# Attention score products on 64 rows each, with q stored without zero padding

## The chip, the cores and the metric

The kernel runs on one core of a Trainium2 chip. The metric is device time in microseconds, from the first to the last instruction of one execution. The kernel before was run three times; the median is 1041.5 us. TensorE is called PE in the rows, its weight loads PEld, VectorE DVE, ScalarE ACT, GpSimd POOL, and the engine that issues the transfers SP.

## The reference, cut to what matters

Two batches with eight heads of 576 tokens and 64 dimensions go through two attentions that are added: one over tokens averaged in fours (144 of them), one local, in which a token sees those less than four positions away. Two layers of expert products follow.

```python
q_d = q.reshape(B, H, Sd, factor, D).mean(axis=3)      # k_d, v_d in the same way
out_d = sm_attn(q_d, k_d, v_d)                         # softmax(scale * q k^T) v
out_up = np.repeat(out_d, factor, axis=2)
mask = np.abs(pos[:, None] - pos[None, :]) < factor
scores = np.where(mask, scale * np.matmul(q, k.transpose(0, 1, 3, 2)), -1000000000.0)
...
x = attn_out.transpose(0, 2, 1, 3).reshape(B * S, H * D)
x = _moe_ref(x=x, **moe_kwargs)                        # silu(x @ w_gate) * (x @ w_val) @ w_out
return _moe2_ref(x=x, **moe2_kwargs)                   # eight experts, routed by a balanced softmax
```

## The kernel before, in words

**The attention** (L362 to L517) works on eight pairs of heads. A pair fills the 128 partitions: the even head has partitions 0 to 63 of q and k (transposed, 576 columns), the odd head 64 to 127. `load_pair` (L309) loads k into one of three buffers and q into one of three fixed tiles `qz`. Such a tile has room for two copies of the 576 columns: copy 0 holds the even head and zeros in partitions 64 to 127, copy 1 the odd head and zeros in partitions 0 to 63. The zeros are written once, by six memsets on GpSimd (L111, L112); each load writes the two other quarters with a transfer of its own (L313, L314).

`pooled` (L369) scales k on ScalarE (L373) and sums k and q over groups of four tokens on VectorE (L374, L381); since q's tile holds two copies, its sum reads 1152 columns.

`scores(h)` (L392) takes two PSUM banks for a head. A product with an identity first writes the mask into each bank (L397, L402). Five window products of 128 by 128 are added to it (L400, L404), with q as the stationary operand: all 128 partitions of copy j, so the other head's half of k meets zeros. Two products of 72 rows with the pooled k follow (L406). All these products but the mask are fp32. Then VectorE takes the extreme of each row (L409 to L411), ScalarE the exponential with its sum (L415 to L421), VectorE the reciprocals (L423, L424), and GpSimd scales the rows (L426, L428). `turn(h)` (L431) transposes the result on TensorE (L437 to L441) and ScalarE copies it out (L443 to L445). `combine(pr)` (L448) multiplies with the values of both heads (L457, L465), adds the upsampled part (L468, L474) and splits the sum into two 16-bit parts (helper L165 to L170). Scores, transposes and combine share six PSUM banks, two for each of them at a time.

**The order.** The generator in L481 to L517 writes it down: scores of the first four heads; then for each head its transposes, the scores of the head four further on, and behind each odd head the combine. The loads of the pair three further on come behind the odd head's scores (L489, L490). From this order and the dependencies a scheduler makes each engine's list at build time by modelled durations, so an engine may take a later instruction first; on the chip each engine follows its list. Transfers are all issued by SP, in one list. Those of gate weights and of pooled values are tied behind the last load of q (`gate(loaded[-1])`, L215, L321).

**Around it** the first layer's weights arrive as 64-bit floats, whose words VectorE and ScalarE turn into fp32 (L189) and then into two 16-bit parts. `conv_gv`, `prep_gv` and three early steps of gate/value products (`gv_step`) are put between the heads (L673 to L682); the rest of that layer follows, and then the eight experts. All products of those layers are issued in L177.

Of the kernel before, what the change touches and what calls it, by code (L numbers as in the profile page):

```python
# [7 lines left out]
F32 = mybir.dt.float32  # L8
# [4 lines left out]
ALU = mybir.AluOpType  # L13
AX = mybir.AxisListType
# [3 lines left out]
B, H, S, D = 2, 8, 576, 64  # L18
FAC, SD = 4, 144
# [3 lines left out]
P = 128  # L23
NPAIR = 4
HS = SD // 2
# [3 lines left out]
WSTART = (0, 120, 240, 360, 448)  # L29
WCUT = (0, 124, 244, 364, 484, 576)  # L30
NW = 5
# [6 lines left out]
DW = 2 * SD  # L38
# [12 lines left out]
NQ = 3  # L51
V4B = 4
NSHORT = NPAIR
QDV = (0, 1, 2, 3, 4, 5, 6, 7)
# [4 lines left out]
def tile_kernel(ctx, tc, qT, kT, vw, vd4, wgv, wo, wg2, w1, w2, out):  # L59
    nc = tc.nc  # L60
    V, A, G, T = nc.vector, nc.scalar, nc.gpsimd, nc.tensor
# [7 lines left out]
    ap = ctxA.enter_context(tc.tile_pool(name="ap", bufs=2, side="right"))  # L69
# [28 lines left out]
    identb = ap.tile([P, P], BF16, tag="identb", bufs=1, name="identb")  # L98
    V.tensor_scalar(identb, dist, 0.0, None, op0=ALU.is_equal)
    maskb = ap.tile([P, 4, P], BF16, tag="maskb", bufs=1, name="maskb")  # L100
# [1 line left out]
                    op0=ALU.is_ge, op1=ALU.mult)  # L102
    ident = cp.tile([P, P], F32, name="ident")
    built.append(V.tensor_scalar(ident, dist, 0.0, None, op0=ALU.is_equal))
    qz = [ap.tile([P, 2, S], F32, tag=f"qz{i}", bufs=1, name=f"qz{i}") for i in range(NQ)]
    vz = [ap.tile([P, NW, 2, P], F32, tag=f"vz{i}", bufs=1, name=f"vz{i}") for i in range(2)]
    vdz = [ap.tile([HS, 2, 2, P], F32, tag=f"vdz{i}", bufs=1, name=f"vdz{i}") for i in range(2)]
    stm = [ap.tile([P, 8], F32, tag=f"stm{i}", bufs=1, name=f"stm{i}") for i in range(2)]
    sts = [ap.tile([P, 8, 2], F32, tag=f"sts{i}", bufs=1, name=f"sts{i}") for i in range(2)]
    for i in range(NQ):  # L110
        G.memset(qz[i][64:, 0], 0.0)  # L111
        G.memset(qz[i][:64, 1], 0.0)  # L112
    for i in range(2):
        V.memset(stm[i], 0.0)
        V.memset(sts[i][:, :, 0], 1.0)
# [190 lines left out]
    ld = {}  # L306
    loaded = []

    def load_pair(pr):  # L309
        k = ap.tile([P, S], F32, tag="k", bufs=NQ, name=f"k{pr}")  # L310
        nc.sync.dma_start(k, kT[pr])
        q = qz[pr % NQ]
        nc.sync.dma_start(q[:64, 0], qT[pr, :64])  # L313
        loaded.append(nc.sync.dma_start(q[64:, 1], qT[pr, 64:]))  # L314
        ld[pr] = k

    v4s = {}
# [44 lines left out]
    def attention():  # L362

        def bank(nm):
            return [psa.tile([P, 512], F32, tag="att", bufs=6, name=f"{nm}_{i}") for i in range(2)]

        qd, kd, exs, ats = {}, {}, {}, {}

        def pooled(pr):  # L369
            q, k = qz[pr % NQ], ld[pr]  # L370
            qd[pr] = ap.tile([P, 2, SD], F32, tag="qd", name=f"qd{pr}")
            kd[pr] = ap.tile([P, SD], F32, tag="kd", name=f"kd{pr}")
            A.activation(k, k, AF.Copy, scale=-0.125)  # L373
            V.tensor_reduce(kd[pr], k.rearrange("p (s a) -> p s a", a=FAC), axis=AX.X, op=ALU.add)  # L374
            A.activation(kd[pr], kd[pr], AF.Copy, scale=1.0 / (FAC * FAC))
            if pr not in QDV:
                t = ap.tile([P, 2, 2 * SD], F32, tag="qt", bufs=1, name=f"qt{pr}")
                G.tensor_tensor(t, q[:, :, 0::2], q[:, :, 1::2], op=ALU.add)
                G.tensor_tensor(qd[pr], t[:, :, 0::2], t[:, :, 1::2], op=ALU.add)
            else:  # L380
                V.tensor_reduce(qd[pr], q.rearrange("p j (s a) -> p j s a", a=FAC), axis=AX.X, op=ALU.add)  # L381

        def pooled_v(pr):
            v4, vd = v4s[pr], vdz[pr % 2]
# [3 lines left out]
            for j in range(2):  # L388
                h = slice(64 * j, 64 * j + 64)
                G.tensor_tensor(vd[:, :, j, h], vt[:, 0, :, h], vt[:, 1, :, h], op=ALU.add)  # L390

        def scores(h):  # L392
            pr, j = h // 2, h % 2
            q, k = qz[pr % NQ], ld[pr]
            nm = f"{h}"
            ps = bank(f"s{nm}")
            T.matmul(ps[0], lhsT=identb, rhs=maskb.rearrange("p u w -> p (u w)"), start=True, stop=False)  # L397
            for w in range(NW - 1):
                ws = slice(WSTART[w], WSTART[w] + P)
                T.matmul(ps[0][:, w * P:(w + 1) * P], lhsT=q[:, j, ws], rhs=k[:, ws],  # L400
                         start=False, stop=w == NW - 2)
            T.matmul(ps[1][:, DW:DW + P], lhsT=identb, rhs=maskb[:, 0], start=True, stop=False)  # L402
            ws = slice(WSTART[4], WSTART[4] + P)
            T.matmul(ps[1][:, DW:DW + P], lhsT=q[:, j, ws], rhs=k[:, ws], start=False, stop=True)  # L404
            for t in range(2):
                T.matmul(ps[1][:HS, t * SD:(t + 1) * SD], lhsT=qd[pr][:, j, t * HS:(t + 1) * HS],  # L406
                         rhs=kd[pr], start=True, stop=True)
            mx, sm = stm[h % 2], sts[h % 2]
            V.tensor_reduce(mx[:, :4], ps[0].rearrange("p (u w) -> p u w", u=4), axis=AX.X, op=ALU.min)  # L409
            V.tensor_reduce(mx[:, 4:5], ps[1][:, DW:DW + P], axis=AX.X, op=ALU.min)  # L410
            V.tensor_reduce(mx[:HS, 5:7], ps[1][:HS, :DW].rearrange("p (u w) -> p u w", u=2),  # L411
                            axis=AX.X, op=ALU.min)
            ex = ap.tile([P, NW * P + DW], F32, tag="ex", bufs=6, name=f"ex{nm}")
            for w in range(4):
                A.activation(ex[:, w * P:(w + 1) * P], ps[0][:, w * P:(w + 1) * P], AF.Exp, scale=-1.0,  # L415
                             bias=mx[:, w:w + 1], accum_out=sm[:, w, 0:1])
            A.activation(ex[:, DO - P:DO], ps[1][:, DW:DW + P], AF.Exp, scale=-1.0,
                         bias=mx[:, 4:5], accum_out=sm[:, 4, 0:1])
            for t in range(2):
                A.activation(ex[:HS, DO + t * SD:DO + (t + 1) * SD], ps[1][:HS, t * SD:(t + 1) * SD], AF.Exp,  # L420
                             scale=-1.0, bias=mx[:HS, 5 + t:6 + t], accum_out=sm[:HS, 5 + t, 0:1])  # L421
            rs = ap.tile([P, 8], F32, tag="rs", name=f"rs{nm}")
            V.tensor_reduce(rs, sm, axis=AX.X, op=ALU.add)  # L423
            V.reciprocal(rs, rs)  # L424
            x = ex[:, :DO].rearrange("p (w k) -> p w k", w=NW)
            G.tensor_tensor(x, x, rs[:, :NW, None].to_broadcast([P, NW, P]), op=ALU.mult)  # L426
            x = ex[:HS, DO:].rearrange("p (t k) -> p t k", t=2)
            G.tensor_tensor(x, x, rs[:HS, 5:7, None].to_broadcast([HS, 2, SD]), op=ALU.mult)  # L428
            exs[h] = ex
# [53 lines left out]
        def start(h):  # L483
            if h < NH:
                if h % 2 == 0:
                    with tc.issue_after(built[0].ins), tc.issue_after(built[1].ins):
                        pooled(h // 2)
                scores(h)
                if h % 2 and h // 2 + NQ < NPAIR * B:  # L489
                    load_pair(h // 2 + NQ)  # L490
# [8 lines left out]
        for h in range(NH):  # L499
# [4 lines left out]
            if h % 2:  # L504
                pr = h // 2
# [157 lines left out]


    load_pair(0)
    load_pair(1)
    load_pair(2)
    load_v(0)
# [4 lines left out]
    for n, _ in enumerate(attention()):  # L673
        pr, r = divmod(n - AHEAD - 5, 6)
        if n == AHEAD:
            conv_gv(0)
        if r == 0 and pr >= 0:
            if pr in EARLY:
                gv_step(0, EARLY.index(pr), True)
            if pr % 2:  # L680
                prep_gv(pr // 2, x1_done[pr])
                conv_gv(pr // 2 + 1, x1_done[pr])  # L682
# [179 lines left out]
```

## Time and profile before

| | us |
|---|---|
| median of 3 runs | 1041.5 |
| lowest and highest | 1039.41 and 1043.37 |
| span of the profiled execution | 1041.1 |
| PE busy in it | 1013.4 |
| DVE busy in it | 756.6 |
| ACT busy in it | 457.7 |
| POOL busy in it | 81.3 |

The profiled execution's own time is the span, from its first to its last instruction. A busy time is the union of an engine's instructions. Matmuls overlap, so that distances between their starts say more of PE's pace than their durations. In the rows, L400 is line 400 of the kernel before, `s<-k,qz` an instruction that writes tile s and reads k and qz, `x8` a count; `<-` behind an idle time names what ended it.

### The profile page before, as it was taken

What the parts mean: (1) busy time and instruction counts of PE and PEld (TensorE: products, weight loads), DVE (VectorE), ACT (ScalarE), POOL (GpSimd) and SP (SyncE); (2) the same over time, 40 slices, a digit from 0 to 9 for tenths busy, and PEclk for the clock granted to TensorE, in tenths of its full rate; (3) what the DMA queues carried; (4) which work ended last, traced back from release to release, by engine and by line L of the source; (5) the groups of instructions that cost most, each with busy time, mean ns of one, the idle gap of its engine ahead of it and who ended that gap; (6) DMA issues with size and microseconds to landing.
All of it is one profiled execution on the core that took longest, in us unless ns stands there. A gap on an engine that the chain in (4) does not pass through costs nothing.

```text
span 1041.1 us, 16454 instructions
## 1 busy us (share of the span) xinstructions
PE 1013.4 (97%) x6540; PEld 651.0 (63%) x6541; DVE 756.6 (73%) x1555; ACT 457.7 (44%) x957; POOL 81.3 (8%) x117
## 2 busy tenths in 40 slices
PE   5989899999999999999999999999999999999998
PEld 4978465666577756566655755656565575665644
DVE  6787888965683999797679749749866973974721
ACT  6797576656351746235135215413522631441300
POOL 5664000000000200000000000000000000000000
PEclk8999899999999999999999999999999999999999
DMA  9542242330020022013012110201201211020011
GB/s 213 156 145 68 81 163 92 151 122 1 1 81 2 1 82 95 28 41 122 1 41 82 41 41 16 107 1 41 96 27 41 81 42 41 1 82 1 1 41 51
DMA packets 22459, 65.54 MB, mean 63 GB/s; under 512 B 12080, under 2 KB 12336, under 8 KB 15984
## 3 DMA queue, kind: packets, MB, share of 16 engines
q1 hardware_dynamic: 22384, 64.51, 18.1%
q8 instruction: 51, 0.84, 0.3%
q14 instruction: 24, 0.20, 0.1%
HBM read 62.14 MB, written 2.36 MB: 62 GB/s over the span
## 4 chain that ended last, share of the span: by engine, by line
PE 85%; DVE 7%; DMA 3%; ACT 3%; issue 1%; SPq 0%; ACTq 0%; DVEq 0%
PE y L177 36%; PE p L177 30%; PE gv L177 10%; PE wo L177 4%; DMA rawg<-in_wgv 2%; PE s L400 1%; PE o L465 1%; DMA k<-in_kT 1%; DVE w L170 1%; DMA rawo<-in_wo 1%; PE lgps L593 1%; DVE cvg L204 0%; DVE mxw L146 0%; PE o L457 0%; PE t L437 0%
## 5 line engine op out<-in xcount | busy, mean ns | idle before, releaser
L177 PE MATMUL y<-w,hhl 128*128 128x512 f16 (+1 forms) x1752 | 396.2, 376 | 0.0
L177 PE MATMUL p<-bop,w 128*128 128x320 f16 (+1 forms) x2688 | 354.4, 286 | 0.8 <-DVE u L734 0.7
L177 PEld LDWEIGHTS <-w 128*128 128x128 f16 x2688 | 263.0, 98 | 90.6 <-issue 1.3
L177 PEld LDWEIGHTS <-hhl 128*128 128x128 f16 x1752 | 171.5, 98 | 178.1
L762 ACT ACTIVATE hhl<-h 128x640 f16<-128x640 f32 (+1 forms) x128 | 83.3, 676 | 159.9 <-DVE h L734 159.8
L177 PE MATMUL gv<-xhl,gv 128*128 128x320 f16 (+1 forms) x864 | 144.3, 329 | 2.9 <-ACT gv L169 2.3
L169 ACT ACTIVATE w<-r,s_w 128x256 f16<-128x256 f32 (+1 forms) x96 | 71.2, 783 | 118.0 <-PE y L177 86.3
L177 PEld LDWEIGHTS <-gv 128*128 128x128 f16 x864 | 84.9, 99 | 58.8 <-issue 3.5
L793 DVE SCALAR_TENSOR_TENSOR acc<-y,pe,acc 128x512 f32<-128x512 f32 (+1 forms) x64 | 47.3, 739 | 101.3 <-PE y L177 100.5
L763 DVE SCALAR_TENSOR_TENSOR hhl<-h,hhl 128x640 f16<-128x640 f32 (+1 forms) x128 | 94.4, 752 | 15.3 <-ACT hhl L762 14.0
L734 DVE SCALAR_TENSOR_TENSOR h<-p,u 128x256 f32<-128x256 f32 (+1 forms) x192 | 84.9, 452 | 19.8 <-PE p L177 14.1
L170 DVE SCALAR_TENSOR_TENSOR w<-r,s_w,w 128x256 f16<-128x256 f32 (+1 forms) x96 | 78.0, 831 | 16.8 <-ACT w L169 16.7
L177 PE MATMUL wo<-ahl,wo 128*128 128x320 f16 (+1 forms) x432 | 73.9, 333 | 0.0
L169 ACT ACTIVATE w<-cmb,s_w 128x512 f16<-128x512 f32 x64 | 43.0, 710 | 42.1 <-DVE cmb L274 40.0
L177 PEld LDWEIGHTS <-wo 128*128 128x128 f16 x432 | 43.3, 101 | 28.2
L734 DVE SCALAR_TENSOR_TENSOR u<-p,u 128x320 f32<-128x320 f32 (+1 forms) x128 | 57.2, 447 | 4.1 <-PE p L177 3.2
L156 POOL PARTITION_ALL_REDUCE g_w<-gm_w x16 | 6.3, 392 | 592.7 <-DVE gm_w L152 586.8
L751 ACT ACTIVATE s<-p 128x256 f32<-128x256 f32 (+1 forms) x64 | 25.4, 397 | 56.9 <-PE p L177 56.9
L146 DVE TENSOR_REDUCE mxw<-r 128x1 f32<-128x1024 f32 x32 | 37.4, 1213 | 12.8 <-DMA r<-in_w 12.8
L170 DVE SCALAR_TENSOR_TENSOR w<-cmb,s_w,w 128x512 f16<-128x512 f32 x64 | 45.9, 739 | 0.1
L294 ACT ACTIVATE j<-r 128x1024 f16<-128x1024 f32 x32 | 33.4, 1045 | 24.5 <-DMA r<-in_w 24.5
L170 DVE SCALAR_TENSOR_TENSOR ahl<-act,sc,ahl 128x512 f16<-128x512 f32 (+1 forms) x24 | 19.6, 818 | 17.6 <-ACT ahl L169 17.6
(203 smaller groups left out, 937.9 us busy)
## 6 DMA issues: line engine op xcount, KB each, us to landing
r<-in_w SPq DMA_DIRECT2D x32, 1024.0 KB, 4.8
rawg<-in_wgv SPq DMA_DIRECT2D x12, 1024.0 KB, 4.8
rawo<-in_wo SPq DMA_DIRECT2D x6, 1024.0 KB, 6.3
vz<-in_vw SPq DMA_DIRECT2D x16, 160.0 KB, 3.2
k<-in_kT SPq DMA_DIRECT2D x8, 288.0 KB, 4.3
qz<-in_qT SPq DMA_DIRECT2D x16, 144.0 KB, 5.2
v<-in_vd SPq DMA_DIRECT2D x8, 288.0 KB
out<-acc SPq DMA_DIRECT2D x8, 256.0 KB, 2.0
```

The costliest lines, as they stand in the source:

```text
L146: V.tensor_reduce(o, i, axis=axis, op=ALU.max, apply_absolute_value=True)
L169: return (A.activation(hi, src, AF.Copy, scale=s), V.scalar_tensor_tensor(lo, src, s, hi, op0=ALU.mult, op1=ALU.subtract))
L170: V.scalar_tensor_tensor(lo, src, s, hi, op0=ALU.mult, op1=ALU.subtract))
L177: T.matmul(ps, lhsT=wf(i, k), rhs=xf(j, k), start=n == 0, stop=n == 3 * nk - 1)
L294: A.activation(junk, t[:, 2 * j:2 * j + 2].rearrange("p a n -> p (a n)"), AF.Abs, accum_out=mx[:, 2 * i + j:2 * i + j + 1])
L400: T.matmul(ps[0][:, w * P:(w + 1) * P], lhsT=q[:, j, ws], rhs=k[:, ws], start=False, stop=w == NW - 2)
L465: T.matmul(dst, lhsT=v[:, w, j], rhs=ats[2 * pr + j][:, off:off + hi - lo], start=j == 0, stop=j == 1)
L734: V.scalar_tensor_tensor(o, ps, HSC, u, op0=ALU.mult, op1=ALU.add)
L751: A.activation(s1, p1, AF.Copy, scale=HSC)
L762: ra = A.activation(t[:, 0], h, AF.Relu)
L763: rv = V.scalar_tensor_tensor(t[:, 1], h, 0.0, t[:, 0], op0=ALU.max, op1=ALU.subtract)
L793: V.scalar_tensor_tensor(acc[t][:, ds], ps, p[:, t:t + 1], acc[t][:, ds], op0=ALU.mult, op1=ALU.add)
```

## The change

A q tile loses its second copy and its zeros, and one transfer loads both heads. The sum over four tokens reads 576 columns. The products of a pair's two heads are issued together, ahead of the even head's softmax: the masks of both heads, then window by window the even head's product on partitions 0 to 63 and the odd head's on 64 to 127, each into its own head's bank, then the pooled products in the same way. The pair takes four banks at once. The softmax of each head stays where it was.

```diff
-    qz = [ap.tile([P, 2, S], F32, tag=f"qz{i}", bufs=1, name=f"qz{i}") for i in range(NQ)]
+    qz = [ap.tile([P, S], F32, tag=f"qz{i}", bufs=1, name=f"qz{i}") for i in range(NQ)]
...
-    for i in range(NQ):
-        G.memset(qz[i][64:, 0], 0.0)
-        G.memset(qz[i][:64, 1], 0.0)
...
-        nc.sync.dma_start(q[:64, 0], qT[pr, :64])
-        loaded.append(nc.sync.dma_start(q[64:, 1], qT[pr, 64:]))
+        loaded.append(nc.sync.dma_start(q, qT[pr]))
...
-            qd[pr] = ap.tile([P, 2, SD], F32, tag="qd", name=f"qd{pr}")
+            qd[pr] = ap.tile([P, SD], F32, tag="qd", name=f"qd{pr}")
...
+            V.tensor_reduce(qd[pr], q.rearrange("p (s a) -> p s a", a=FAC), axis=AX.X, op=ALU.add)
...
+        def products(pr):
+            q, k = qz[pr % NQ], ld[pr]
+            pss = [bank(f"s{2 * pr + j}") for j in range(2)]
+            hd = [slice(64 * j, 64 * j + 64) for j in range(2)]
+            for ps in pss:
+                T.matmul(ps[0], lhsT=identb, rhs=maskb.rearrange("p u w -> p (u w)"), start=True, stop=False)
+            for ps in pss:
+                T.matmul(ps[1][:, DW:DW + P], lhsT=identb, rhs=maskb[:, 0], start=True, stop=False)
+            for w in range(NW):
+                ws = slice(WSTART[w], WSTART[w] + P)
+                for ps, h in zip(pss, hd):
+                    o = ps[0][:, w * P:(w + 1) * P] if w < 4 else ps[1][:, DW:DW + P]
+                    T.matmul(o, lhsT=q[h, ws], rhs=k[h, ws], start=False, stop=w > 2)
+            for t in range(2):
+                for ps, h in zip(pss, hd):
+                    T.matmul(ps[1][:HS, t * SD:(t + 1) * SD], lhsT=qd[pr][h, t * HS:(t + 1) * HS],
+                             rhs=kd[pr][h], start=True, stop=True)
+            return pss
+
         def scores(h):
-            pr, j = h // 2, h % 2
...
+            pr = h // 2
+            if h % 2 == 0:
+                pss[pr] = products(pr)
+            nm, ps = f"{h}", pss[pr][h % 2]
```

## Rows read from the trace of the kernel before

**Rows 1.** the profile's page, part 1: busy us, share of the span, instructions

```profile
PE 1013.4 (97%) x6540; PEld 651.0 (63%) x6541; DVE 756.6 (73%) x1555; ACT 457.7 (44%) x957; POOL 81.3 (8%) x117
```

**Rows 2.** by stretch: busy us of PE, PEld, DVE, ACT, POOL; granted clock; DMA share; GB/s

```profile
0.00:28.00 28.00, 15.92 (x89) 12.93 (x90) 17.23 (x45) 17.94 (x76) 17.15 (x35) 0.88 0.92 210
28.00:66.00 38.00, 33.77 (x324) 31.67 (x324) 29.77 (x71) 32.10 (x132) 22.03 (x26) 1.00 0.57 160
66.00:108.40 42.40, 42.40 (x332) 35.68 (x331) 33.89 (x85) 34.15 (x125) 22.80 (x25) 1.00 0.24 74
108.40:142.00 33.60, 28.39 (x168) 16.93 (x167) 28.94 (x54) 21.12 (x32) 1.97 (x3) 0.90 0.33 125
...
331.00:1041.00 710.00, 705.93 (x4470) 437.15 (x4468) 514.81 (x1064) 252.34 (x424) 12.19 (x21) 1.00 0.12 46
```

**Rows 3.** chain of waits, 0 to 28 us: start, us, what

```profile
11.51 7.18 DMA k<-in_kT
19.22 9.03 DMA rawg<-in_wgv
```

**Rows 4.** chain of waits, 66 to 108.4 us, its shares by line

```profile
by line: PE gv L177 24.5%; PE o L465 21.8%; PE s L400 11.0%; PE o L457 10.6%; PE t L437 8.9%; PE s L406 6.1%; PE t L441 4.8%; PE s L404 3.3%; PE s L397 2.9%; PE t L438 2.1%; DVE act L554 1.8%; PE sm_gv L162 1.5%; PE sm_gv L160 1.2%; PE sm_v
```

**Rows 5.** PE's groups by line, 28 to 108.4 us; last row 66 to 108.4

```profile
L400 PE MATMUL s<-k,qz 128*128 128x128 f32 x88 | 11.8, 275 | 0.1
...
L400 PE MATMUL s<-k,qz 128*128 128x128 f32 x40 | 5.5, 276 | 0.0
```

**Rows 6.** PE in order of time, 66 to 76 us: start, us, instructions merged

```profile
65.88 1.05 PE L400 MATMUL s<-k,qz 128*128 128x128 f32 x8
66.77 0.22 PE L402 MATMUL s<-maskb,identb 128*128 128x128 bf16 x1
66.82 0.44 PE L404 MATMUL s<-k,qz 128*128 128x128 f32 x2
67.10 0.65 PE L406 MATMUL s<-kd,qd 128*72 128x144 f32 x4
...
72.00 0.42 PE L441 MATMUL t<-ident,ex 72*72 72x72 f32 x4
```

**Rows 7.** weight loads from 70.35 us; forms of the combine's tile o

```profile
70.25 0.53 PEld L465 LDWEIGHTS o<-at,vz 128*128 128x128 f32 x4
...
L465 PE MATMUL o<-at,vz x160: 252/275/347, 34.8 to 110.5; 128*128 128x120 f32 x96, 128*128 128x124 f32 x32, 128*128 128x92 f32 x32
```

**Rows 8.** PE in order of time, 72.4 to 73.4 us

```profile
72.47 0.38 PE L400 MATMUL s<-k,qz 128*128 128x128 f32 x2
72.78 0.38 PE L162 MATMUL sm_v<-gr_v,ones 1*128 1x1 f32 x2
73.09 0.49 PE L400 MATMUL s<-k,qz 128*128 128x128 f32 x2
```

**Rows 9.** DVE's groups by line, 28 to 108.4 us

```profile
L381 DVE TENSOR_REDUCE qd<-qz 128x288 f32<-128x1152 f32 x4 | 5.3, 1336 | 0.0
...
L374 DVE TENSOR_REDUCE kd<-k 128x144 f32<-128x576 f32 x4 | 2.9, 736 | 0.0
```

**Rows 10.** instructions on q's tile qz: ns min/median/max, first and last start

```profile
L314 SPq DMA_DIRECT2D qz<-in_qT x8: 471/537/597, 1.8 to 53.0; - x8
...
L111 POOL MEMSET qz<- x3: 572/572/572, 0.7 to 3.2; 64x576 f32 x3
```

**Rows 11.** waits of SP's queue, 0 to 66 us: total, times, longest

```profile
SPq L313 <- PE s L406: 12.4, 4, 8.5
```

**Rows 12.** chain of waits, 28 to 66 us

```profile
45.45 7.45 DMA rawg<-in_wgv
58.03 1.39 ACT ex L415 x8
```

**Rows 13.** waits of all engines, 28 to 108.4 us: total, times, longest

```profile
ACT cvg L201 <- DMA rawg<-in_wgv: 5.3, 2, 3.4
...
PE s L397 <- DVE x L474: 0.8, 1, 0.8
```

More of the change, by code (lines that the diff above doesn't have):

```diff
@@ L365, in bank @@
             return [psa.tile([P, 512], F32, tag="att", bufs=6, name=f"{nm}_{i}") for i in range(2)]
-        qd, kd, exs, ats = {}, {}, {}, {}
+        qd, kd, exs, ats, pss = {}, {}, {}, {}, {}
         def pooled(pr):
             q, k = qz[pr % NQ], ld[pr]
-            qd[pr] = ap.tile([P, 2, SD], F32, tag="qd", name=f"qd{pr}")
+            qd[pr] = ap.tile([P, SD], F32, tag="qd", name=f"qd{pr}")
             kd[pr] = ap.tile([P, SD], F32, tag="kd", name=f"kd{pr}")
@@ L375, in pooled @@
             A.activation(kd[pr], kd[pr], AF.Copy, scale=1.0 / (FAC * FAC))
[L376 to L381, printed above, removed]
+            V.tensor_reduce(qd[pr], q.rearrange("p (s a) -> p s a", a=FAC), axis=AX.X, op=ALU.add)
         def pooled_v(pr):
@@ L390, in pooled_v @@
                 G.tensor_tensor(vd[:, :, j, h], vt[:, 0, :, h], vt[:, 1, :, h], op=ALU.add)
-        def scores(h):
-            pr, j = h // 2, h % 2
[L394 to L407, printed above, removed]
+        def products(pr):
[16 more added lines that the diff above has]
+            return pss
+        def scores(h):
+            pr = h // 2
+            if h % 2 == 0:
+                pss[pr] = products(pr)
+            nm, ps = f"{h}", pss[pr][h % 2]
             mx, sm = stm[h % 2], sts[h % 2]
```

## The prediction, made before the result was known

> **What bounds the kernel now.** I read the page first, then the span by stage, then the chain of waits inside each stage, and last the instructions of the score products. The page [rows 1] has PE busy 97% of the span, so at first sight every PE saving counts. The stages [rows 2] say where that may be believed. From 331 us on, PE is busy 705.93 of 710 us with expert products that the diff leaves alone. The diff lies in the attention, from 0 to about 108 us, and its three parts have different limits. In 0 to 28 the DMA engines are busy 92% of the time, and the chain [rows 3] is two transfers, 7.18 us for a k and 9.03 us for the first gate weight. In 28 to 66 PE (33.77 of 38 us), DVE (29.77) and ACT (32.10) are all nearly full, and none of them alone sets the end. In 66 to 108.4 PE is busy for the whole 42.40 us, and the chain [rows 4] is almost nothing but PE: gate/value products put in early (24.5%), combine, transposes, and the score products (L397 to L406, 23%). Behind the attention, in 108.4 to 142, PE is idle 5 of 33.6 us while DVE, busy 28.94, converts weights. So a microsecond of PE counts fully in 66 to 108.4, partly in 28 to 66, hardly before 28; and behind 108.4 it must be accepted by DVE.
>
> **The score products.** One fp32 product is two weight loads and two matmuls in the trace. In the stretch from 28 to 108.4 there are 88 matmuls of L400, of 128 in all, thus 5.5 of the 8 pairs, 16 to a pair [rows 5]. Their durations overlap, so I go by distances between starts [rows 6]: eight of L400 from 65.88 to 66.77, 0.111 us each; four of L406 take 0.65 us at 0.287 each, so (0.65 - 0.287) / 3 = 0.121 from start to start. A pair has 20 window and 8 pooled matmuls: 20 x 0.111 + 8 x 0.121 = 3.2 us. The number of instructions stays as it is; what is new is that each uses 64 rows, and that two of them on different rows may run at once.
>
> No row has two matmuls of 64 rows, so I bound the distance. Upper end: nothing overlaps, 0.111 and no gain. Lower end: the least distance I find for 128 columns, 0.05 us from the mask product at 66.77 to the next start at 66.82 [rows 6], which is half and worth 1.6 us a pair. What speaks for the upper end is the weight load. In L465 the last four products of a pair stream 92 columns and not 120, yet four loads of 128 columns run from 70.25 for 0.53 us at 192 ns each [rows 7], (0.53 - 0.19)/3 = 0.113 apart: there the load sets the pace, not the stream. And L162, whose weights are a single row and whose stream is one column, still takes 0.31 us for two, from 72.78 to 73.09 [rows 8]. So fewer rows make nothing faster, and all rests on two loads going on side by side. I take the lower end: the two streams use different rows and different banks, and in the smallest fp32 products, L441, distances do fall with the columns (72 by 72: four in 0.42 us at 0.23 each, 0.063 apart [rows 6]), so no fixed cost per instruction holds 0.111 up. It is the weakest step, and the upper end stays in the range.
>
> The Trainium skill, "TensorEngine Tiling (Array Packing)", section Key Properties, says that different tiles of the array can load weights and multiply in parallel; by that the gain is the 1.6 us, whereas the rows on L465 and L162, read alone, give none. No run here shows it.
>
> **Changes of shape.** Before the products stand masks on 128 rows, behind them again 128 rows. A change between the full array and a smaller piece of it has a price in the trace. Two matmuls of L400 start at 72.47, the next start would be due at 72.69, and L162 (one row) starts at 72.78; back on 128 rows, the next two L400 take 0.49 us where two take 0.38 [rows 8]. So 0.09 of waiting and 0.11 of a load that nothing hides: 0.2 a change, 0.4 a pair. It is nothing if 64 rows are not treated so, and 0.8 if another product is scheduled into the middle of a pair. Net on PE: 1.6 - 0.4 = 1.2 us a pair.
>
> **What of it is on the path.** 66 to 108.4 has 40 matmuls of L400 [rows 5], 2.5 pairs: 2.5 x 1.2 = 3.0 us, all on the path. The 3 pairs of 28 to 66 save 3.6, of which I count half, 1.8, since ACT and DVE are as full there. The 2.5 pairs before 28 count nothing: PE is busy 15.92 of 28 us, and the transfers cover it.
>
> **The other edits.** The sum over four tokens reads 576 columns in place of 1152: L381 falls from 1336 ns to the 736 of L374, which has just that shape, 0.6 us for each of eight pairs, 4.8 of DVE. Four of them stand behind 28 us [rows 9], the others before it, under the transfers; the four are 2.4 us of a full DVE, and are what lets DVE follow PE's half gain in 28 to 66, so I do not add them again. The six memsets of q, 0.57 us each on POOL, with the last of L111 started at 3.2 us [rows 10], lie under the first transfers; they cost nothing now and give nothing. Eight fewer issues of about 0.5 us each on SP [rows 10] start the first loads up to 0.5 us earlier, under a DMA that is full with the same bytes: nothing. Later SP waits for PE, not PE for SP [rows 11].
>
> **Moved.** The odd head's products come ahead of the even head's softmax. The loads of the pair three ahead wait for them (L313 <- PE s, 12.4 us for four [rows 11]) and so start earlier, and with them the gate weight queued behind, whose second transfer (45.45, 7.45 us) is on the chain [rows 12] and kept ACT waiting (5.3 us for two, 3.4 the longest [rows 13]). I count none of it; it is the upside below. The odd head's two banks are held longer, which is the downside.
>
> **Sum.** 3.0 + 1.8 = 4.8; DVE behind 108.4 swallows perhaps 0.5: 4.3 us. The profiled span is 1041.1, 0.4 under the median of 1041.5, with next to nothing around it. 1041.1 - 4.3 = 1036.8, 1037.2 from the median: I say 1037.0.
>
> **Rivals.** (a) **The two heads do not run at once**, so the change does not do what it says. Then PE pays 0.4 x 2.5 = 1.0 and half of 0.4 x 3 = 0.6; DVE's 2.4 gives half back. 1041.1 + 1.6 - 1.2 = 1041.5. For it: the load's pace [rows 7, 8].
>
> (b) **Everything falls into place**: all 5.5 pairs count, 6.6, and the second gate weight is no longer waited for, another 2 to 3: 1041.1 - 9 = 1032. For it: that wait is the largest of ACT's; and odd scores are ready early, so ACT is seldom short of work. Against: ACT is busy 32.10 of 38 us already.
>
> (c) **ACT takes over.** PE is faster, but ACT, busy 34.15 of 42.4 [rows 2], empties the banks no faster. If it holds the pace from 66 to 108.4, the 3.0 us there are lost and 1.8 less the 0.5 are left: 1041.1 - 1.3 = 1039.8. The Trainium skill, "TensorEngine Tiling (Array Packing)", section PSUM Bottleneck, says just this, that packing speeds TensorE and not the emptying of PSUM; the stages agree so far as ACT's share goes.
>
> (d) **Slower: the six banks.** A pair of scores now takes four of them at once, and transposes and combine share what is left. The transposes of the next pair can get the odd head's banks only when its seven exponentials are done, 0.35 us each (eight records in 1.39 us [rows 12]), 2.4 us. If PE reaches them first and has nothing else to do, that is up to 2.4 us a pair, 2 x 5.5 = 11, less the 4.3: 1041.1 + 6.7 = 1048. It decides when PE finishes the combine before ACT finishes the odd exponentials. Against it: the one wait of PE for a bank that counts today is 0.8 us, L397 for DVE's x [rows 13].
>
> **How the numbers follow.** Chances: forecast 0.33, (a) 0.16, (b) 0.23, (c) 0.11, (d) 0.17. A measurement here can tell about 0.5%, 5.2 us. Faster than that are nearly all of (b) and half of the forecast's own spread (1034 to 1039): 0.38. Slower are most of (d): 0.16. The same: 0.46. The range runs from 1029.5 (b with the transfers kinder still) to 1045 (part of d); it leaves out the ends of (b) and (d), under 2 in 10. The forecast's own range is 1034 to 1039.
>
> **What would show it.** In the changed profile L400 and L406 would come at some 0.055 us from start to start, a pair's scores taking under 2.5 us with masks and changes; at 0.11 the main step is wrong. The sum for q would be near 0.73 us. The span from 66 us to the last combine should be 3 us shorter with PE still the chain; if PE waits before L437 for ACT's L415 or L420, it is (d); if the chain there goes through ACT, (c). A second gate weight issued before 45 us would be the start of (b). The forecast is wrong if the attention does not end earlier, or if what it gains is idle PE time before 142 us.

## The result, and the profile after

The changed kernel takes 1054.77 us (median of 4 runs, 1050.27 to 1063.06), the kernel before 1042.25 (median of 4 runs): ratio 1.0129, 95% interval 1.0092 to 1.0166. It is slower by some 12 us, where 1037.0 was forecast and 1045 was the end of the range. The four runs follow the granted clock: 1050.27 us at 0.982, 1051.19 at 0.979, 1058.35 at 0.973, 1063.06 at 0.969. From the first to the last it is 0.013 of the clock, which over some 1056 us makes 27 us more at half clock; where TensorE is busy, that is worth up to 14 us (an estimate), and the runs lie 12.8 apart. The profiled run is the first of these, so the trace below holds 7.4 us of loss (a span of 1048.5 against 1041.1); of the other 5 us of the median only the clock of the runs is known.

The page, part 1, answers to [rows 1]:

```profile
PE 1021.0 (97%) x6541; PEld 650.1 (62%) x6541; DVE 751.2 (72%) x1555; ACT 458.7 (44%) x957; POOL 73.8 (7%) x111
```

DVE is busy 5.4 us less than before, about what the narrower sum should make it, and POOL 7.5, of which the six missing memsets of 0.57 us are 3.4. PE is busy 7.6 us more, with as many instructions but for one record.

The stages, with the columns of [rows 2]:

```profile
0.00:28.00 28.00, 15.95 (x94) 10.82 (x95) 15.16 (x46) 20.31 (x86) 15.49 (x31) 0.78 0.79 210
28.00:66.00 38.00, 36.77 (x263) 31.25 (x262) 23.85 (x62) 26.11 (x112) 16.22 (x20) 0.81 0.49 149
66.00:108.40 42.40, 41.33 (x329) 31.93 (x329) 30.58 (x79) 34.42 (x128) 22.12 (x28) 1.00 0.29 83
```

Look at 28 to 66. PE is busy 36.77 us, more than the 33.77 of before, with 263 matmuls in place of 324; DVE and ACT do a fifth less. PE is slower here, and the number behind POOL says by what: the granted clock is 0.81 where it was 1.00. Cut where the clock changes, two stages stand out:

```profile
15.50:28.00 12.50, 6.12 (x25) 4.89 (x26) 6.69 (x18) 11.73 (x55) 11.56 (x16) 0.50 0.63 180
28.00:42.80 14.80, 14.80 (x82) 12.93 (x80) 7.09 (x16) 7.05 (x31) 5.79 (x9) 0.50 0.26 80
```

PE is at 1.2 GHz from 15.5 to 42.8 us. It fell while PE stood idle (7.94 us before the transposes at 21.88, until POOL had scaled the first exponentials), as it does in before; but there the low stretch is 20.5 to 27.3. Here PE is busy without a gap from 28.00 to 42.80 and still gets half the clock: work worth 7.4 us takes 14.8. The transposes of head 2 start at 43.7 us, against 37.0 in before: 6.7 us lost. Those of head 12 start at 103.8 against 95.9, the 100th gate/value product at 138.7 against 129.8, and the experts begin 7.4 us late (their first activation at 339.7 against 332.3). After that nothing moves: from 331 to 1041 us the granted clock is 1.00 in both.

Up to that 100th product the clock is nearly all of the loss. PE is busy at 1.2 GHz for 24.9 us there, in before for 7.7; half of the difference, 8.6 us, is an estimate of what it costs, and 8.8 are lost. PE's idle time is 0.4 us less than in before. The loss shrinks to 7.4 us because before has another low stretch further on, 6.9 us of busy PE from 307.2, and the changed kernel has 3.4 us from 315.9.

PE in order of time, with one pair whose heads alternate and one whose heads do not:

```profile
44.48 0.60 PE L388 MATMUL s<-maskb,identb 128*128 128x512 bf16 x2
...
45.74 0.94 PE L395 MATMUL s<-k,qz 64*128 64x128 f32 x12
46.61 0.28 PE L390 MATMUL s<-maskb,identb 128*128 128x128 bf16 x2
...
53.15 0.38 PE L388 MATMUL s<-maskb,identb 128*128 128x512 bf16 x1
53.46 1.16 PE L395 MATMUL s<-k,qz 64*128 64x128 f32 x8
54.55 0.39 PE L388 MATMUL s<-maskb,identb 128*128 128x512 bf16 x1
54.87 1.16 PE L395 MATMUL s<-k,qz 64*128 64x128 f32 x8
55.95 0.23 PE L390 MATMUL s<-maskb,identb 128*128 128x128 bf16 x1
56.11 0.48 PE L395 MATMUL s<-k,qz 64*128 64x128 f32 x2
...
58.08 0.66 PE L436 MATMUL t<-ident,ex 128*128 128x128 f32 x4
```

From 45.74 twelve matmuls take 0.94 us: two heads at once. From 53.46 eight on one half take 1.16 us, no faster than the eight of 128 rows in [rows 6], which took 1.05. The written order says "in turn" for all pairs, but the scheduler's list follows modelled durations and free banks: pairs 2, 4, 5 and 6 are issued head by head, masks and products of the one, then of the other. Such a pair costs 58.08 - 53.15 = 4.93 us; in before a head took from 65.66 to 67.59, so a pair 3.86.

The last pair alternates, but stands in two parts:

```profile
90.94 0.60 PE L388 MATMUL s<-maskb,identb 128*128 128x512 bf16 x2
91.46 1.16 PE L395 MATMUL s<-k,qz 64*128 64x128 f32 x14
92.55 2.76 PE L174 MATMUL gv<-xhl,gv 128*128 128x512 f16 x12
95.15 0.27 PE L390 MATMUL s<-maskb,identb 128*128 128x128 bf16 x2
```

Between the products for its first banks and those for its second, PE's list has 12 gate/value products; the exponentials of head 14 start at 96.0 us, not 90.7.

### The profile page after: what moved, and what is told of

It is laid out like the page before. It is cut to its first block, busy times and chain, and to the rows that moved or that the text cites. A ratio compares the mean times of both kernels' runs of the same rounds, so it can differ in the third digit from the quotient of the medians.

```text
span 1048.5 us, 16420 instructions
## 1 busy us (share of the span) xinstructions
PE 1021.0 (97%) x6541; PEld 650.1 (62%) x6541; DVE 751.2 (72%) x1555; ACT 458.7 (44%) x957; POOL 73.8 (7%) x111
## 4 chain that ended last, share of the span: by engine, by line
PE 82%; DVE 9%; ACT 5%; DMA 3%; issue 2%; POOL 0%; SPq 0%; ACTq 0%; DVEq 0%
PE y L174 36%; PE p L174 29%; PE gv L174 7%; PE wo L174 4%; PE s L395 1%; DMA rawg<-in_wgv 1%; PE o L464 1%; DVE w L167 1%; DMA rawo<-in_wo 1%; DMA k<-in_kT 1%; ACT rawg L217 1%; ACT ex L414 1%; PE vv L342 1%; PE lgps L592 0%; PE t L436 0%
## 5 line engine op out<-in xcount | busy, mean ns | idle before, releaser
L174 PEld LDWEIGHTS <-w 128*128 128x128 f16 x2688 | 263.0, 98 | 90.7 <-issue 1.3
L762 DVE SCALAR_TENSOR_TENSOR hhl<-h,hhl 128x640 f16<-128x640 f32 (+1 forms) x128 | 94.4, 752 | 14.8 <-ACT hhl L761 13.2
L174 PEld LDWEIGHTS <-wo 128*128 128x128 f16 x432 | 42.8, 100 | 27.7
L291 ACT ACTIVATE j<-r 128x1024 f16<-128x1024 f32 x32 | 33.4, 1045 | 24.8 <-DMA r<-in_w 24.8
```

Of the source, the lines that this page charges most:

```text
L174: T.matmul(ps, lhsT=wf(i, k), rhs=xf(j, k), start=n == 0, stop=n == 3 * nk - 1)
L291: A.activation(junk, t[:, 2 * j:2 * j + 2].rearrange("p a n -> p (a n)"), AF.Abs, accum_out=mx[:, 2 * i + j:2 * i + j + 1])
L762: rv = V.scalar_tensor_tensor(t[:, 1], h, 0.0, t[:, 0], op0=ALU.max, op1=ALU.subtract)
```

## The experiments

Sixteen kernels were run. The times of before beside them were 1042.06 to 1042.70 us, so the ratios compare.

| kernel | us | ratio, 95% interval |
|---|---|---|
| pair_padded | 1045.81 | 1.0031 [1.0013, 1.0049] |
| rows64_alone | 1050.68 | 1.0083 [1.0056, 1.0111] |
| in_turn_forced | 1049.32 | 1.0066 [1.0045, 1.0086] |
| clock_held | 1060.75 | 1.0166 [1.0114, 1.0217] |
| in_turn_scores_first | 1046.71 | 1.0040 [1.0028, 1.0052] |
| hybrid | 1050.23 | 1.0073 [1.0050, 1.0096] |
| hybrid_scores_first | 1047.53 | 1.0043 [1.0025, 1.0061] |
| order_last_only | 1043.68 | 1.0014 [1.0000, 1.0029] |
| order_first_only | 1046.46 | 1.0042 [1.0027, 1.0057] |
| in_turn_middle | 1045.74 | 1.0030 [1.0017, 1.0043] |
| before_combine_first | 1055.23 | 1.0121 [1.0099, 1.0143] |
| padded_combine_first | 1057.12 | 1.0151 [1.0130, 1.0171] |
| hybrid_combine_first | 1064.32 | 1.0208 [1.0193, 1.0224] |
| in_turn_combine_first | 1067.63 | 1.0240 [1.0217, 1.0264] |

The two clock probes put work of their own ahead of the kernel (1374.2 and 1447.0 us) and are not in the table.

**The order alone, and the 64 rows alone.** pair_padded keeps the padding and the 128 rows, and writes the products as the change does; rows64_alone drops the padding and keeps the written order of before.

```diff
+            for j, ps in enumerate(pss):
...
+                T.matmul(o, lhsT=q[:, j, ws], rhs=k[:, ws], start=False, stop=w > 2)
```

> The kernel before with its zero padding (128 rows, two q copies), but the products of a pair's two heads issued together as in the change. Theory A (64 rows are what costs: changes of shape between mask and product, a clock that stays at 1.2 GHz longer over them): no 64-row work, so within 3 us of before, about 1042, and the clock back at 2.4 GHz before 30 us. Theory B (the new order costs: four banks at once, odd transposes late): most of the loss stays, 1048 to 1055.

```diff
-                T.matmul(ps[0][:, w * P:(w + 1) * P], lhsT=q[:, j, ws], rhs=k[:, ws],
+                T.matmul(ps[0][:, w * P:(w + 1) * P], lhsT=q[hd, ws], rhs=k[hd, ws],
```

> The changed kernel's q (one copy, 64 rows per product) in the order of the kernel before, head by head, two banks at a time. Theory A: four changes of shape a head, 0.2 us each, 11 heads behind 28 us: 8.8 us of TensorE more, less 2.4 us of VectorE; 1046 to 1052. Theory B: the order is the old one, so 1038 to 1043.

The order costs 3.2 us by itself, between what the theories gave it. The 64 rows cost 8.1 without any change of order, and their trace shows the low clock again: 1.2 GHz from 19.7 to 43.6 us, head 2's transposes at 44.0. So the early loss goes with the 64 rows and not with the order. Theory A's four changes of shape a head are in the 8.1 us too (it gave 1046 to 1052), and this run does not part them from the clock.

**All pairs in turn.** in_turn_forced ties every product of a pair behind the one written before it.

```diff
+            def mm(*a, **kw):
+                nonlocal last
+                with gate(last):
+                    last = T.matmul(*a, **kw)
```

> The changed kernel with its score products tied in the written order, so that all eight pairs alternate (in the changed kernel four pairs do, four run head after head with a mask between). Theory A1 (the lost alternation is the loss): a pair's scores take 2.5 us in place of 4.9, four pairs give back 9 us of TensorE, about 6 of it on the path: 1040 to 1044. Theory A2 (the low clock from 16 to 43 us is the loss): only what alternation adds from 44 us on, and the clock stays low as long: 1046 to 1052. Theory B: order and banks as in the changed kernel, 1048 to 1055.

PE in order of time, one pair:

```profile
63.67 0.75 PE L392 MATMUL s<-maskb,identb 128*128 128x512 bf16 x3
64.65 0.22 PE L392 MATMUL s<-maskb,identb 128*128 128x128 bf16 x1 [0.23 <-ACT at L451]
64.80 1.39 PE L392 MATMUL s<-k,qz 64*128 64x128 f32 x20
66.02 0.66 PE L392 MATMUL s<-kd,qd 64*72 64x144 f32 x8
66.60 0.66 PE L443 MATMUL t<-ident,ex 128*128 128x128 f32 x4
```

66.60 - 63.67 less the wait of 0.23 is 2.70 us, 1.16 less than before's 3.86. That is the forecast's 1.2 a pair. The splits were worth 1054.8 - 1049.3 = 5.5 us. Yet with eight such pairs the kernel is 1049.32 - 1042.61 = 6.7 us slower than before. Two rows of its trace, with the columns of [rows 2]:

```profile
14.60:31.70 17.10, 9.93 (x69) 7.96 (x66) 9.03 (x21) 11.95 (x55) 12.43 (x17) 0.50 0.60 187
35.10:41.90 6.80, 6.80 (x29) 5.99 (x30) 1.81 (x7) 4.32 (x24) 4.53 (x6) 0.50 0.04 11
```

With two more low stretches, 59.0 to 62.4 and 89.7 to 93.1, PE is busy 23.5 us at 1.2 GHz before 108.4 us, in before 3.2. Half of the difference, 10 us by estimate, is more than the eight pairs gain (8 x 1.16 = 9.3). From 28 to 108.4 us PE is also idle 9.5 us, in before 4.2. So a low clock is not bound to products on one half: here all pairs are in turn.

**Is it the clock?** clock_held adds 36 products of zeros, 128x512, in PE's early idle stretch; clock_probe puts segments of products of its own ahead of the kernel before.

```diff
+                    for _ in range(36):
+                        T.matmul(pw2, lhsT=warm[:, :P], rhs=warm, start=True, stop=True)
```

> The changed kernel with 36 matmuls of zeros (128x512, 16 bit, into a spare bank) put into TensorE's idle time between the scores of the first four heads and the first transposes. Theory A2: the clock stays at 2.4 GHz, the products, the v squares and the first combine (22 to 43 us, about 21 us at 1.2 GHz) take half the time where TensorE sets the pace: 5 to 9 us less than the changed kernel, 1043 to 1048, and the spread between runs shrinks. Theory A1 or B: 0 to 2 us less.

It held the clock to 28 us (1.00 in that stage), and then PE lost it all the same, from 29.0 to 42.7 and from 63.2 to 87.1 us, in the second stretch while busy 23.90 of 23.90 us. The first fall lies in an idle time of 6.5 us before the transposes at 32.46. With 1053.57 to 1064.26 us the kernel is no faster than the change: a miss.

```diff
+    for _ in range(180):
+        one(pw, fn[:64])
+        one(pv, fn[64:])
```

> The kernel before with a probe ahead of its attention: blocks of 100 dense 16-bit 128x512 products, and between them about 40 us each of (1) 180 fp32 128x128 products on 128 rows, (2) the same on 64 rows, all on one half, (3) 360 on 64 rows, halves in turn, (4) 720 16-bit 128x128 products on 72 rows, (5) four fp32 products on 64 rows and one 16-bit product on 128 rows, forty times. TensorE is never idle. Theory C (fewer active rows bring the clock down): it holds 2.4 GHz in 1, falls to 1.2 within 2, and perhaps in 4 and 5; in 3, with both halves at work, it holds. Theory I (only idle time brings it down): 2.4 GHz from end to end. Time of the whole: 1042 plus about 330 us.

Its stretches, with the columns of [rows 2]: 128 rows, 64 rows of one half, two halves in turn:

```profile
25.30:65.30 40.00, 40.00 (x360) 40.00 (x359) 0.00 (x0) 0.00 (x0) 0.00 (x0) 1.00 0.00 1
87.20:127.30 40.10, 40.10 (x360) 40.10 (x360) 0.00 (x0) 0.00 (x0) 0.00 (x0) 1.00 0.00 1
149.30:189.40 40.10, 40.10 (x719) 40.10 (x720) 0.00 (x0) 0.00 (x0) 0.00 (x0) 1.00 0.01 2
```

Count over time: 0.111 us a matmul on 128 rows, 0.111 on one half, 0.056 in turn. The clock stays at 1.00 in all three, so these 40 us of dense work on 64 rows did not bring it down. That seemed to clear the 64 rows. The probe had asked only half the question: each segment began at full clock.

> The kernel before with six runs of products of its own put ahead, each after about 12 us in which TensorE stands idle: 300 on 128 rows in fp32, 300 on one half of 64 rows, 600 on the two halves in turn, 30 times four on 64 rows and a 16-bit 128x512 one, 600 on 72 rows in 16 bits, and 75 of 128x512. It shows after how many us of work the clock comes back up. Theory C2 (products on half the rows do not bring the clock back up, as in the changed kernel, where it stayed at 1.2 GHz until 42.8 us although TensorE was busy from 28 on): the runs on 64 rows stay at 1.2 GHz for their whole length or at least twice as long as the one on 128 rows. Theory I2 (any dense work brings it back): it rises within the same time, to 2 us, in all of them.

The second probe sets some 8 us of idle PE before each segment (a chain on VectorE that rewrites the operand). Its stretches, cut where the clock changes: 128 rows (two), one half, both halves in turn (two):

```profile
34.20:39.20 5.00, 5.00 (x24) 5.00 (x25) 0.26 (x1) 0.00 (x0) 0.00 (x0) 0.51 0.00 0
39.20:103.40 64.20, 64.20 (x578) 64.20 (x577) 0.00 (x0) 0.00 (x0) 0.00 (x0) 1.00 0.01 1
112.20:240.00 127.80, 127.80 (x599) 127.80 (x600) 0.17 (x1) 0.00 (x0) 0.00 (x0) 0.50 0.00 1
248.80:254.10 5.30, 5.30 (x50) 5.30 (x52) 0.27 (x1) 0.00 (x0) 0.00 (x0) 0.50 0.00 0
254.10:318.00 63.90, 63.90 (x1148) 63.90 (x1148) 0.00 (x0) 0.00 (x0) 0.00 (x0) 1.00 0.01 2
```

This is the plainest result of the study. On 128 rows the clock is back after 5.0 us, in turn after 5.3. On one half it does not come back: 127.8 us at 0.50, with PE busy in every one of them. Theory C2 holds for one half alone, not for two halves in turn; each segment ran once, in one execution. The segments after these ran among the kernel's own products and tell nothing of the clock's return.

**Early pairs as before.** hybrid keeps pairs 0 to 2 padded and head by head, and puts pairs 3 to 7 on 64 rows, tied in turn.

```diff
+            if pr >= NQ:
+                if j == 0:
+                    pss[pr] = products(pr)
+                ps = pss[pr][j]
+            else:
+                ps = padded(pr, j)
```

> Pairs 0 to 2 as in the kernel before (zero padding, 128 rows, head by head), pairs 3 to 7 from one q copy on 64 rows, in turn, tied. Clock theory: no 64-row work before 40 us, so the clock is back at 2.4 GHz by about 28 us as in the kernel before, and of in_turn_forced's loss of 4.4 us by the second pair's transposes none is left: 1043 to 1046; the end stays as slow as there. Rival (the loss is the order alone, not the clock): as in_turn_forced, 1048 to 1050.

The early loss is gone: the first low stretch ends at 27.9 us, and head 2's transposes come at 36.4 (before 37.0). Head 10's come at 86.1, as in before (86.2), although PE had less to do: a second low stretch runs from 55.2 to 62.0, with PE busy 6.5 us, behind a wait of 2.4 us. Head 14's come at 107.5 against 100.2, so a further loss sits behind 86 us, where the clock is 1.00. PE's waits there, 28 to 108.4 us (total, times, longest):

```profile
PE o L498 <- ACT ex L456: 3.8, 2, 2.4
PE s L407 <- ACT at L484: 1.5, 1, 1.5
```

In before, PE waits 0.3 us for exponentials in that whole stretch. Here the combine (tile o) waits 3.8 us until ACT has emptied a bank of scores, and products wait for the banks of transposes.

**The early gate/value products.** Two kernels put them behind the last pairs' scores.

```diff
-EARLY = (4, 6, 7)
+EARLY = (5, 6, 7)
...
+                with gate(scored[-1]):
+                    gv_step(0, EARLY.index(pr), True)
```

> in_turn_forced with the early gate/value steps put behind the last pair's score products (steps after pairs 5, 6, 7 and not 4, 6, 7, and tied behind those products). Theory: in the new order the last pair's four banks come late, TensorE takes 12 early gate/value products between its masks and its products, and the last softmaxes start at 97 us in place of 91: put first, they give back 3 to 5 us: 1044 to 1046.5. Rival (the end is slow for another reason): 1048 to 1050.

> hybrid with the early gate/value steps behind the last pair's scores, tied. If the low clock in the first half and the late last pair are the two losses, both are gone here and what is left is the gain of the in-turn products and of the smaller sum: 1037 to 1042. If one of them stands: 1043 to 1047.

Worth 2 to 3 us each: the exponentials of head 14 start at 90.3 in the first of them, not 97.1. Its time is just above what was expected; the hybrid misses the 1037 to 1042 by 5 us, and the 1043 to 1047 of one loss left by half a microsecond. Both stay slower than before, with the waits for banks in place (2.3 and 3.5 us of the combine for exponentials).

**Where the order costs.** Padded, 128 rows, the products together only in the last two pairs, or only in the first six.

```diff
-            if pr > 5:
+            if pr < 6:
                 if j == 0:
                     pss[pr] = products(pr)
```

> The kernel before with its zero padding and 128 rows; only in the last two pairs (heads 12 to 15) are the products of both heads written together. With all eight pairs written so, the padded kernel took 1045.8 us against 1042.6. Theory E (what the order costs is lost at the end, because the last pair takes four banks at once and its softmaxes begin late): about as slow as that, 1044.5 to 1047, with the 100th product of gv more than 3 us later than the 129.8 us of before. Theory M (it is lost over the pairs in the middle): 1041.5 to 1043.5, and the 100th product of gv within 1.5 us of before.

> The other half of the same question: zero padding and 128 rows, both heads' products together in pairs 0 to 5, heads 12 to 15 one at a time as before. Theory E: 1041.5 to 1043.5, the 100th product of gv within 1.5 us of 129.8. Theory M: 1044.5 to 1047. If both of these kernels come out slower than before by about half of 3.2 us, the cost lies in every pair alike.

The last two pairs cost 1.0 us (the interval reaches down to nothing), the first six 3.8: theory E, the end, falls, and it is the pairs ahead of it. PE's waits for ACT, 28 to 108.4 us, in pair_padded (two rows), order_first_only (two) and order_last_only (one):

```profile
PE o L464 <- ACT ex L422: 2.2, 2, 1.9
PE o L472 <- ACT ex L427: 0.9, 1, 0.9
```

```profile
PE o L484 <- ACT ex L442: 3.0, 2, 1.8
PE o L492 <- ACT ex L447: 0.9, 1, 0.9
```

```profile
PE o L484 <- ACT at L472: 1.1, 1, 1.1
```

Their sums, 3.1, 3.9 and 1.1 us, rank like the three losses, 3.2, 3.8 and 1.0. Two heads written together fill four of six banks at once, and the combine waits until ACT has emptied one. But these waits do not explain the losses. The traced executions lost other amounts: their spans are 6.2, 3.4 and 0.2 us above before's. And before has a wait of its own in that stretch, which the first two kernels no longer have and the third has at 1.8 us:

```profile
PE sm_gv L162 <- DVE gr_gv L161: 2.7, 1, 2.7
```

So PE's whole idle time from 28 to 108.4 us is 4.2 us in before and 3.1, 4.7 and 3.4 us in the three. What the three have there, and before has not, is a low clock (in the same order, columns of [rows 2]):

```profile
57.60:61.00 3.40, 3.20 (x15) 3.20 (x16) 2.72 (x6) 3.40 (x20) 0.18 (x1) 0.51 0.67 248
34.80:41.60 6.80, 6.10 (x28) 6.10 (x29) 4.39 (x10) 6.80 (x31) 2.83 (x5) 0.50 0.20 59
55.40:58.80 3.40, 3.40 (x18) 3.40 (x18) 3.40 (x9) 3.40 (x19) 0.45 (x1) 0.50 0.93 327
```

In pair_padded it is low for another 2.2 us from 28. Half of the busy time at low clock, 2.7, 3.1 and 1.7 us by estimate, ranks like the losses too. In the first two the clock fell in or behind a wait for exponentials, in the third behind the 1.8 us for DVE; in before 2.7 us of waiting brought no fall. So the banks may cost by the clock what they do not cost in idle time, and no run parts the two.

**Only the middle in turn.** Pairs 3 to 5 on 64 rows, tied, q tiles of their own; all others as before.

```diff
+            if 3 <= pr < 6:
+                loaded.append(nc.sync.dma_start(qh[pr % NQ], qT[pr]))
```

> The kernel before, with only pairs 3 to 5 on unpadded q (tiles of their own), their products tied in turn on 64 rows; pairs 0 to 2 and 6 and 7 padded and head by head. Theory E (the gain of products in turn is real, and what the change lost lies in the pairs that are split by the order, in the low clock at the start and in the order of the last pairs): head 10's transposes come near 82 to 84 us instead of 86.2, and the time is 1037 to 1040, faster than before. Theory X (between 28 and 90 us ACT and DVE set the pace as soon as PE gains anything, so that products in turn are worth nothing there): head 10's transposes again near 86 us and 1041 to 1044.

The first low stretch is as long as in before (21.5 to 28.4), a second runs from 55.7 to 59.1, behind a wait of 2.0 us, three pairs gain 1.16 each, and the time is 3.0 us over before, at 1042.75 to 1048.99. Head 10's transposes do come early, at 82.2 us, so theory X is wrong about the middle; head 12's come late, at 98.8 against 95.9. PE's waits:

```profile
PE o L499 <- ACT ex L457: 3.8, 3, 2.0
PE s L408 <- ACT at L485: 1.6, 2, 1.1
PE o L507 <- ACT at L485: 1.0, 1, 1.0
```

That is 6.4 us of waits for ACT and its banks against 3 x 1.16 = 3.5 of gain. All idle time of PE from 28 to 108.4 us is 7.3 us, 3.1 more than in before, and the second low stretch, 3.4 us of busy PE, costs some 1.7. In the profiled execution, one of the two shortest of twelve, PE makes part of it good behind the attention (its span is 1041.0 us), so the rows explain that nothing is gained. The 3.0 us of the median go with the clock: eight of the twelve runs have a granted clock of 0.987 or less, of 25 runs of before beside them none is under 0.988, and the four at 0.989 or 0.990 took 1042.75 to 1044.29 us.

**Giving the combine its banks earlier.** The combine is written ahead of the next pair's products; one kernel does only that to the kernel before.

```diff
-            start(h + AHEAD)
-            yield
...
+                yield
+                start(h + AHEAD - 1)
+                start(h + AHEAD)
```

> A control: the kernel before, with nothing changed but the place of the combine (its banks taken ahead of the next pair's). In before TensorE waits 0.3 us in all for exponentials from 28 to 108.4 us, so there is nothing to gain from banks: 1042 to 1046 by either theory. If this is faster than before by 2 us or more, the place of the combine is worth something by itself, and the three other runs are to be read against this one.

> Zero padding, 128 rows, both heads' products together in all eight pairs, as in the run that took 1045.8 us; but each pair's combine takes its two banks before the next pair's products take theirs, and both heads of those products are started behind it. Theory S (3.2 us of the order's cost are TensorE's waits for exponentials before the combine, because the combine takes the bank that the newest products have just filled): between 28 and 108.4 us those waits go from 3.1 us to under 1, and the time is 1042 to 1044. Theory L (two heads at once leave too little other work while their softmaxes run, whatever banks they take): waits of 2 us or more remain, before the transposes or the combines, and the time is 1045 or more.

> Pairs 0 to 2 padded and head by head, pairs 3 to 7 on unpadded q, in turn on 64 rows and tied; with the combine's banks taken ahead of the next pair's products. The same kernel without that took 1050.2 us, with 3.8 us of waits for exponentials before the combine and 2.3 us before products. Theory S: 1040 to 1044, the shortest with products in turn, and below before if the turn is then worth anything. Theory L: 1046 to 1050.

> The changed kernel with all eight pairs tied in turn, the early products of gv behind the last pairs' scores (this took 1046.7 us), and the combine's banks taken ahead of the next pair's products. Theory S: TensorE's waits for ACT before combines and products, 7 us of them between 28 and 108.4, fall below 3, and the time is 1041 to 1044; what is left over before is the clock at 1.2 GHz in the first 60 us. Theory L: 1045 to 1049.

The control alone is 13 us slower, and that spoils the test: the edit also starts both heads' products later against the transposes, and in the control's trace the clock is low from 20.8 to 37.9 us (before to 27.3). Against their control the padded kernel loses 1.9 us, the two in turn 9 and 12. In padded_combine_first the combine's wait for exponentials is gone, but one for the copies of the transposes stands in its place:

```profile
PE o L464 <- ACT at L452: 4.8, 3, 3.1
```

So theory S got one of its numbers, that wait, and none of its times. That the banks cause the order's cost is argued from wait rows, and the clock stands beside them as a rival; no run had the banks at full clock, and so the cause stays open. A seventh bank was not tried: the other two are held as a pair by the early gate/value products. No kernel of the study beats before.

## Why the prediction was wrong

**The distance** was right. The weakest step, that two heads run at once, holds: 0.056 us a matmul in turn against 0.111. The Trainium skill, "TensorEngine Tiling (Array Packing)", section Key Properties, said so of different tiles of the array, and the trace agrees. The upper end, no gain, holds for products on the same half. Rival (a) did not occur in the hardware, but in four pairs of eight it did in the schedule.

**Changes of shape** is the first step that failed. The price was about right, 0.3 us out and back where I took 0.4. On the way in, it is 0.32 us from the mask to the first product (54.55 to 54.87), in before 0.22 (65.66 to 65.88), and the second product starts 0.21 behind the first and not 0.11 (two from 56.11 take 0.48 us, and one takes 0.27): 0.2 us for loads that nothing hides. On the way out, eight matmuls from 53.46 make the next due at 54.45, and the mask starts at 54.55, 0.1 late. Their number was wrong. I took two a pair and allowed 0.8 us "if another product is scheduled into the middle". A split pair has eight, four out and back, 4 x 0.30 = 1.2 us, and nothing gained against it: 4.93 - 3.86 = 1.07 us lost where 1.2 were to be won. I read the written order as the issued order, though it is a scheduler that makes the list at build time. The same section of the Trainium skill says that a change of tiling mode drains TensorE; the trace agrees so far as the mask comes 0.1 us late.

**What of it is on the path** is the second, and the larger. "The 2.5 pairs before 28 count nothing" and the half gain from 28 to 66 took PE's clock as given, 1.00 in [rows 2]. But 0.88 stood in the row above: the clock falls in the early idle stretch, and when it returns went with what PE did next. With pair 2 head by head on one half from 23.49 to 32.41 us, it returned at 42.8, not 27.3. The sum had no term for it; it was worth 6.7 us by head 2, and the clock is 8.6 of the 8.8 us lost by the 100th gate/value product. In the second probe one half alone did not raise the clock; in the kernel the early loss comes with head-by-head products on 64 rows (rows64_alone, low to 43.6 us) and goes with padded early pairs (hybrid, to 27.9). Why the clock stayed low so long is open in part. Behind 32.41 us PE worked on 128 and 72 rows, and the clock took another 10.4 us, where the probe's 128 rows took 5.0; what the 72-row products did there, no run shows. in_turn_forced had it back at 31.7 and lost it again at 35.1. And hybrid, without the early loss, is no faster than in_turn_forced.

**Rival (d), the six banks,** was right that waits for banks come, and wrong in the place. I looked for them at the transposes, and the combine waits. Its price was up to 2.4 us a pair; measured are 3.1 us in all on 128 rows, in place of a wait of 2.7 in before, and 6.4 with three pairs in turn. In the changed kernel itself these waits are only 0.3 us. Had pairs and clock behaved as I assumed, the gain would probably have met them: in_turn_middle, with three pairs in turn and the early clock of before, is the nearest run to that case, and it is 3.0 us slower. That the forecast would have failed by this step too is argued and not shown, since the clock is lower in that kernel's runs as well.

**Rival (c)** is near to it: banks are emptied no faster. In hybrid PE is busy only 36.72 of the 42.4 us from 66 to 108.4, and the last combine still starts at 113.3 us, not 104.8.

**The small terms** held. The sum for q takes 739 ns (736 forecast), DVE is busy 5.4 us less (4.8 forecast), and the memsets and the issues show nothing. The first gate weight does move ahead, issued at 15.0 us and not 19.2; the second comes later, at 48.7 and not 45.5, as PE is late by then. ACT's wait for them, [rows 13], falls from 5.3 to 1.5 us, and the attention still ends late.

## What to carry to other kernels

Packing two small products side by side halves their time only where they are issued next to each other, so look at the issued list and not at the written one, and count each way out of and back into the packed shape (0.3 us here). Before an engine is made faster, ask which banks the work behind it shares: a pair of heads that is ready together needs its banks together, and here the combine then waited for one of six. Hold all idle time against all idle time, for a new wait can stand where an old one has gone. Where the granted clock stands below 1.00 in a stage, look at which products would have to bring it back.

## What was not expected of the hardware

In these probes one half of the rows kept the full clock and did not get it back. At full clock, 40.1 us of products on one half ran at 1.00 throughout; after an idle stretch of 8.3 us, 127.8 us of the same products, with PE busy all the time, ran at 0.50, 0.213 us each. The two halves in turn brought the clock back after 5.3 us, like 128 rows after 5.0. In the trace the rise shows in the products themselves, in couples of the two halves:

```profile
253.65 0.42 PE L95 MATMUL pw<-fn 64*128 64x128 f32 x1
253.85 0.40 PE L95 MATMUL pv<-fn 64*128 64x128 f32 x1
...
254.32 0.27 PE L95 MATMUL pv<-fn 64*128 64x128 f32 x1
254.32 0.27 PE L95 MATMUL pw<-fn 64*128 64x128 f32 x1
254.43 0.27 PE L95 MATMUL pv<-fn 64*128 64x128 f32 x1
```

A couple starts within 0.01 us, and the next 0.11 us later, where it had been 0.21. The Trainium skill, "TensorE: Matmul & The Clock Gate", section What's actually happening, says that the low clock is the default and that activity releases it; the runs agree for 128 rows and for both halves, and differ for one half, on which a busy engine stayed low; there the measurement decides.
